# Values of eight key tiles at once, downs in half rows behind the gate/up products, and all output projections after the attention, in a fused attention and GEGLU block

## The chip, the cores and the metric

The kernel runs on one core of one Trainium2 chip. The metric is the device time of one execution in microseconds (us). A core has five engines, each with its own instruction queue: TensorE (PE in the profile; its weight loads are shown apart as PEld), VectorE (DVE), ScalarE (ACT), GpSimd (POOL) and SyncE (SP), which here only issues DMA transfers. The engines meet through semaphores. TensorE's array has 128 rows by 128 columns and can be tiled: a product of 64 rows uses the lower or the upper half of the rows, and two such products, one for each half, can run side by side; a product of 32 columns uses a quarter of the columns.

## The reference

All is fp32, with S = 2048 tokens, D = 576, 32 heads of Dh = 18 and F = 4608 hidden columns:

```
xn = layernorm(x)
s  = MHA(xn)                  # softmax(q k^T * Dh**-0.5) v for 32 heads, then @ wo
g  = silu((gelu(xn @ w_gate) * (xn @ w_up)) @ w_down)
out = x + s * g
```

## The kernel before

**Numbers.** Products of fp32 precision are made from split operands: each fp32 value becomes a high and a low part in TensorE's faster fp32r type, and three products (high x high, high x low, low x high) are summed in PSUM. This holds for the projections, the FFN and the scores. The values (probabilities times V) are plain fp32, on four tiles of 32 columns, one for each of four heads.

**Stages.** A prologue normalises x, transposes it, makes q, k and v and stores them in DRAM. Then comes the long part, one stream of 144 *FFN sections* into which the attention is woven. The tokens are in NB = 4 blocks of TB = 512. In each block the hidden width is cut into NR = 18 row blocks of two 128-wide groups, and one section (`section`, L529) is one group: 27 paired steps of gate and up products (each a pair of 64-row products, one on either half of the array; L393), the split of the next section's weights on GpSimd (`split_gu`), and the activation (`activate`, L403): Square on ScalarE (L406), a multiply-add on VectorE (L407), Copy of `up` on ScalarE (L410) and a product on VectorE (L411), Tanh on ScalarE (L412), a last VectorE step (L414). GpSimd splits its result into `hh` and `hl`, which the downs read.

**The attention.** Its 32 units (four heads by one block of tokens) take four sections each, 128 sections in all (`ATT`, L42). `FIRST` (L41) gives 9 lead sections ahead of them, with so many score pairs each, and 7 are left as the tail. In an attention section `spread` (L56) puts 16 more steps between the 27: 8 pairs of products for the maxima (L787, reduced by VectorE at L788) of a later unit, and 8 pairs of scores (L818), whose exponentials ScalarE takes at L819. Together these are 43 paired steps, called G in the prediction.

**Order behind G in an attention section** (main loop, L914 to L938): the maxima's last steps on VectorE in the third section of a unit (`max_neg`, L790); values of four key tiles (`values`, L844, products at L853); the product that turns the maxima around (`max_end`, L798, L801), also in the third section; the tasks of the output projection; in every second section the downs of the finished row block (`downs`, L560); `finish` (L566), which splits the w_down weights.

**Downs** (`down`, L496). For row blocks other than 0, 1, 16 and 17 all of them come at once in half rows (`half_downs`, L445): eight sums `k` (four token tiles by two halves of D) of six steps each. The upper rows go through the sums in the order 0 to 7; the lower rows start with the last two, 6 and 7, and then take 0 to 5, and step by step one product of the lower rows stands beside one of the upper rows. Both halves of a sum go to the same PSUM bank, so the lower half of sums 0 to 5 may begin only when the upper half has ended. `behind` (L439) sees to that: a tiny ScalarE instruction on a `mark` tile (L441) is made to wait for the last product of the upper half, and the first product of the lower half waits for that mark. `add_down` (L420) adds the finished sum to `Y`: VectorE (L425), or ScalarE for row block 0 (L423). Row blocks 0, 1, 16 and 17 go through the full array, 24 products behind each of two sections (L436 too).

**Output projection.** `load_o` (L592), `norm_o` (L611), `load_wo` (L615), `split_o` (L622) and `project_o` (L651) do it for one block after the other as tasks of single sections, through a schedule written out at L694 to L727. For blocks 0 to 2 the 14 products of one place (128 tokens by 288 columns, L661) are woven into a half-row downs stint; those of block 3 lie in the tail and the epilogue (L941 to L996). `gates` (L511) stores silu's factors of a finished block.

**Who sets the order.** TensorE's order is the program's, by hand. The other engines' order within a section comes from the scheduler, save for single instructions held by `keep_in_program_order`. SyncE issues DMAs in its queue's order. PSUM has eight banks, in tags f (2), m (3) and s (3) (`BANKS`, L45); a matmul that needs a bank waits until its last reader is through.

Of the kernel before, what the change touches and what calls it, by code (L numbers as in the profile page):

```python
# [34 lines left out]
VC = NT // NA  # L35
KB, VB = 7, 2
# [4 lines left out]
FIRST = (0, 0, 4, 6, 6, 6, 6, 6, 6)  # L41
# [10 lines left out]
def f(ap):  # L52
    return ap.bitcast(F32)
# [13 lines left out]
def kernel(ctx: ExitStack, tc: tile.TileContext, x, wqkv, wo, w_gate, w_up, w_down, out):  # L67
# [11 lines left out]
    oT = dram.tile([NQ, P, S], F32, name="oT")  # L79
# [297 lines left out]
    FF = {"w": ahead, "xd": XD, "down": [], "gates": [], "n": 0, "po": None,  # L377
# [42 lines left out]
    def add_down(b, r, py, Y, j, c):  # L420
        yy = Y[:, j, 288 * c:288 * c + 288]
        if r == 0:
            nc.scalar.activation(yy, py, AF.Copy)  # L423
        else:
            nc.vector.tensor_tensor(yy, py, yy, op=ALU.add)  # L425
        if b == NB - 1 and r == NR - 1:
            finals.append((Y, j, c))
# [17 lines left out]
    def half_downs(b, r, hs, wd, Y, po=None):  # L445
# [28 lines left out]
        def out_of(a):  # L474
            bank_o, product_o, _ = po
            for i in range(len(OUT)):
                def step(i=i):
                    product_o(bank_o, i, slice(HR * a, HR * a + HR), a == 0 and i == 0, a == 1 and i == len(OUT) - 1)
                yield step
# [12 lines left out]
    def in_halves(due):  # L492

        return due[-2] and 1 < due[1] < NR - 1

    def down(b, r, hs, wd, Y, js, once):  # L496
        last = len(DOWN) - 1
        if once and 1 < r < NR - 1:
            if js[0] == 0:
                half_downs(b, r, hs, wd, Y, FF["po"] or None)  # L500
# [7 lines left out]
        if b < NB - 1 and r == NR - 1:  # L508
            FF["gates"] += [(b, j, c, Y) for j in js for c in range(2)]

    def gates():  # L511

        for k, (b, j, c, Y) in enumerate(FF["gates"]):
            rows, cc = slice(b * TB + j * P, b * TB + (j + 1) * P), slice(288 * c, 288 * c + 288)
            if j >= 2:
                if c == 0:
                    free = op.tile([P, NK * P], F32, name="th", tag=("oh", "ol")[j - 2])
                th = free[:, 288 * c:288 * c + 288]
            elif k < 3:
                th = op.tile([P, 288], F32, name="th", tag=("yy", "yy", "xx")[k], bufs=(2, 2, 1)[k])  # L520
            else:
                th = ffn.tile([P, 288], F32, name="th")
            tc.keep_in_program_order(nc.scalar.activation(th, Y[:, j, cc], AF.Tanh, scale=0.25))
            nc.gpsimd.tensor_scalar(th, th, 1.0, 1.0, op0=ALU.add, op1=ALU.mult)
            nc.gpsimd.tensor_tensor(th, th, Y[:, j, cc], op=ALU.mult)
            nc.sync.dma_start(ys[rows, cc], th)
        FF["gates"] = []

# [31 lines left out]
    def downs():  # L560
        while FF["down"] and (FF["down"][0][-1] < FF["n"] or FF["n"] == NF):
            down(*FF["down"].pop(0)[:-1])
            if FF["down"] and FF["gates"]:
                gates()

    def finish(pool=ffn, cut=split, bufs=1):  # L566
# [8 lines left out]
        if n % G == G - 1:  # L575
# [9 lines left out]
    op = ctx.enter_context(tc.tile_pool(name="op", bufs=1, reuse_waits="tile"))  # L585
    OT = op.tile([P, NK, TB], F32, name="OT")
    OW = [op.tile([P, NK, 288], F32R, name=name) for name in ("woh", "wol")]
    OG = {}
    OUT = [(k, x, w) for k in range(KT) for x, w in ((0, 0), (0, 1), (1, 0))] + [(KT, 0, 0), (KT, 0, 1)]
    HIND = TB // P - 1  # L590

    def load_o(b, k, pool=op, heads=range(H)):  # L592

        toks = slice(b * TB, (b + 1) * TB)
        if ("den", k) not in OG:
            OG["den", k] = pool.tile([P, TB], F32, name="den")
        den = OG["den", k]
        row, end = k * P, min(D, (k + 1) * P)
        while row < end:
            h, d = divmod(row, DH)  # L600
            m = max(1, (end - row) // DH) if d == 0 else 1
            e = min(DH, d + end - row)
            n = m * (e - d)
            rows = slice(row - k * P, row - k * P + n)
            row += n
            if h in heads:
                nc.sync.dma_start(OT[rows, k, :], oT.rearrange("g (a p) t -> (g a) p t", p=32)[h:h + m, 1 + d:1 + e, toks])
                nc.sync.dma_start(den[rows], rT[h:h + m, toks].rearrange("h (o s) -> h o s", o=1)
                                  .to_broadcast([m, e - d, TB]))

    def norm_o(k):  # L611
        n = min(P, D - k * P)
# [9 lines left out]
    def split_o(i, own=None):  # L622
# [8 lines left out]
        if own:  # L631
            kept.append((oh, ol))
# [392 lines left out]
```

## Time and profile before

| | |
|---|---|
| median of 3 runs | 2572.22 us (2572.05 to 2572.49) |
| the profiled execution's own time | 2571.53 us |
| its span in the trace | 2569.7 us |
| TensorE busy | 2563.5 us |
| VectorE, ScalarE, GpSimd busy | 1973.0, 1573.3, 1366.4 us |
| DMA | 327.34 MB, 127 GB/s on average |
| granted TensorE clock | 1.0 |

The page's first part gives the busy time of each engine, the second the span in 40 slices of 64 us (digits are tenths; PEclk is the granted clock of TensorE). The fourth part follows the chain of work that ended last back to the start. Lines of groups read: line, engine, operation, output <- inputs, shapes, count | busy us in total, mean ns of one | us that the engine was idle before them, and what ended the idle time. Lines of a timeline read: start and length in us, engine, line, operation, count, and in brackets the idle time before and who ended it. A window's line gives start:end, its length, TensorE's busy time and instructions in it, the granted clock, the DMA engines' busy share and the GB/s. Line numbers are those of the kernel before.

### The profile page before, as it was taken

Reading aid. Unit: us, or ns where it says so; the run is one execution under the profiler, and the core shown is the slowest. Engines: PE = TensorE matmul, PEld = TensorE weight load, DVE = VectorE, ACT = ScalarE, POOL = GpSimd, SP = SyncE. Lnnn points to the kernel's source line nnn. Section 1 sums busy time; section 2 is a strip of 40 time slices with the busy share of each in tenths; the row PEclk is TensorE's granted clock in tenths of the full one; section 3 lists DMA queues with packets and bytes.
Section 4 is the critical chain, followed back from the end, with each engine's and each line's share of the span. In section 5 each row is a group of like instructions: output and inputs, shape, how many; then the busy total and the mean of one; then the engine's idle time right before and its main releaser. Section 6 shows DMA issues by size and latency. Waiting matters only on the chain.

```text
span 2569.7 us, 62810 instructions
## 1 busy us (share of the span) xinstructions
PE 2563.5 (100%) x23766; PEld 1930.2 (75%) x23766; DVE 1973.0 (77%) x3502; ACT 1573.3 (61%) x3069; POOL 1366.4 (53%) x1506
## 2 busy tenths in 40 slices
PE   9999999999999999999999999999999999999999
PEld 8888777777777777777777777777777777777778
DVE  5326888888887888787888887878888888788445
ACT  3223466666666676666667766666666766676642
POOL 2117545544566455555457555555455845555663
PEclk9999999999999999999999999999999999999999
DMA  8876444443455444544545454445445543544442
GB/s 266 269 238 159 119 107 102 102 111 97 112 129 140 103 115 99 141 110 114 132 114 138 114 129 115 124 107 136 110 109 127 143 110 104 138 120 111 102 121 57
DMA packets 394940, 327.34 MB, mean 127 GB/s; under 512 B 107980, under 2 KB 308684, under 8 KB 394640
## 3 DMA queue, kind: packets, MB, share of 16 engines
q1 hardware_dynamic: 394640, 323.32, 49.9%
q8 instruction: 190, 3.11, 0.5%
q14 instruction: 110, 0.90, 0.1%
HBM read 269.79 MB, written 52.88 MB: 126 GB/s over the span
## 4 chain that ended last, share of the span: by engine, by line
PE 99%; DVE 0%; DMA 0%; ACT 0%; issue 0%
PE pg L393 26%; PE py L436 18%; PE acc L853 18%; PE pe L818 9%; PE pu L393 9%; PE pm L787 9%; PE po L169 7%; PE po L661 3%; PE pt L230 0%; PE pm L801 0%; DMA xx<-in_A_x_dram 0%; DVE bs L198 0%; ACT xth L177 0%; DVE xx L212 0%; DVE st L202 0%
## 5 line engine op out<-in xcount | busy, mean ns | idle before, releaser
L819 ACT ACTIVATE pT<-pe 128x512 f32<-128x512 f32 x2048 | 1150.8, 598 | 305.7 <-PE pm L787 214.9
L788 DVE TENSOR_REDUCE mx<-pm 128x1 f32<-128x512 f32 x2048 | 1250.8, 680 | 67.8 <-PE pm L787 66.0
L393 PE MATMUL pg<-xd,wh 64*128 64x512 f32 x2592 | 930.6, 391 | 0.0
L393 PE MATMUL pu<-xd,wh 64*128 64x512 f32 x2592 | 929.6, 390 | 0.0
L787 PE MATMUL pm<-KS,q 64*128 64x512 f32 x2048 | 785.2, 388 | 0.0
L818 PE MATMUL pe<-q,KS 64*128 64x512 f32 x2048 | 777.1, 387 | 0.0
L393 PEld LDWEIGHTS pg<-xd,wh 64*128 64x128 f32 x2592 | 476.2, 184 | 105.7 <-issue 29.1
L393 PE MATMUL pg<-xd,wl 64*128 64x512 f32 x1296 | 501.6, 387 | 0.0
L393 PE MATMUL pu<-xd,wl 64*128 64x512 f32 x1296 | 501.4, 387 | 0.0
L393 PEld LDWEIGHTS pu<-xd,wh 64*128 64x128 f32 x2592 | 477.1, 184 | 18.9
L853 PE MATMUL acc<-pT,VS 128*32 128x512 f32 x4096 | 466.0, 595 | 0.0
L102 POOL TENSOR_TENSOR wl<-raw,wh 128x384 fp32r<-128x384 f32 x432 | 436.9, 1024 | 13.6
L100 POOL TENSOR_SCALAR hh<-t 128x512 fp32r<-128x512 f32 x128 | 79.1, 618 | 627.3 <-DVE t L414 615.5
L436 PE MATMUL py<-dh,hh 64*128 64x288 f32 (+1 forms) x1968 | 409.8, 298 | 0.0
L425 DVE TENSOR_TENSOR Y<-py,Y 128x288 f32<-128x288 f32 x544 | 242.3, 456 | 217.9 <-PE py L436 209.2
L787 PEld LDWEIGHTS pm<-KS,q 64*128 64x128 f32 x2048 | 375.6, 184 | 42.8 <-DVE mx L788 5.2
L436 PE MATMUL py<-dh,hl 64*128 64x288 f32 (+1 forms) x1968 | 401.0, 292 | 0.0
L436 PE MATMUL py<-dl,hh 64*128 64x288 f32 (+1 forms) x1968 | 400.9, 292 | 0.0
L818 PEld LDWEIGHTS pe<-q,KS 64*128 64x128 f32 x2048 | 369.8, 184 | 33.5
L853 PEld LDWEIGHTS acc<-pT,VS 128*32 128x32 f32 x4096 | 120.5, 109 | 274.5 <-issue 271.2
L436 PEld LDWEIGHTS py<-dh,hh 64*128 64x128 f32 (+1 forms) x1968 | 273.6, 185 | 39.4 <-DVE t L414 19.3
L100 POOL TENSOR_SCALAR wh<-raw 128x384 fp32r<-128x384 f32 x432 | 218.8, 518 | 107.2 <-DMA raw<-in_B_w_up_dram 59.6
(129 smaller groups left out, 3451.8 us busy)
## 6 DMA issues: line engine op xcount, KB each, us to landing
KS<-qk SPq DMA_DIRECT2D x1536, 36.0 KB
raw<-in_B_w_gate_dram SPq DMA_DIRECT2D x144, 288.0 KB
raw<-in_B_w_up_dram SPq DMA_DIRECT2D x144, 288.0 KB
raw<-in_B_w_down_dram SPq DMA_DIRECT2D x68, 576.0 KB
VS<-vs SPq DMA_DIRECT2D x128, 152.0 KB
qk<-t SPq DMA_DIRECT2D x72, 256.0 KB
q<-qk SPq DMA_DIRECT2D x384, 36.0 KB
xd<-xhs SPq DMA_DIRECT2D x24, 384.0 KB
```

Source lines behind the costliest of these rows:

```text
L100: first = nc.gpsimd.tensor_scalar(hi, raw, 1.0, 1.0, op0=ALU.mult, op1=ALU.mult)
L102: low_part[:] = [keep(nc.gpsimd.tensor_tensor(lo, raw, f(hi), op=ALU.subtract))]
L169: nc.tensor.matmul(o, st, m, start=(i == 0), stop=(i == len(terms) - 1))
L393: nc.tensor.matmul(o, w[1 + wp][k][rr, c, :], xd[xp][k][rr, c, :], start=(i == 0), stop=(i == len(terms) - 1))
L425: nc.vector.tensor_tensor(yy, py, yy, op=ALU.add)
L436: return nc.tensor.matmul(py, hs[g][a][rr, j * P:(j + 1) * P], wd[w][rr, g, 288 * c:288 * c + 288], start=start, stop=stop)
L661: nc.tensor.matmul(po, o[x][rr, k, :], ow[w][rr, k, :], start=start, stop=stop)
L787: nc.tensor.matmul(pm, QS[u, r][rr, t * P:(t + 1) * P], KS[(u * NA + c) % KB][r][rr, :], start=True, stop=True)
L788: nc.vector.tensor_reduce(MX[u][:, 2 * r + a, t, c:c + 1], pm, axis=AX.X, op=ALU.max)
L818: nc.tensor.matmul(pe, KS[(u * NA + c) % KB][r][rr, t * P:(t + 1) * P], QS[u, r][rr, :], start=True, stop=True)
L819: nc.scalar.activation(PT[u, kt][:, 2 * r + a, :], pe, AF.Exp, scale=SCALE)
L853: nc.tensor.matmul(ACC[u][32 * a:32 * a + 32, :], VS[(u * NA + c) % VB][:, v:v + 32], pt[:, a, :], start=first, stop=last, skip_group_chec ...
```

## The change

Seven things are changed together.

1. *Values.* They come in every second attention section, for eight key tiles at once (`VV = 2 * VC`), in one PSUM accumulation where two were added before; `pT` has eight buffers in place of four, and the V tiles of two sections are loaded together.
2. *Downs.* All row blocks of the attention sections go in half rows, also 0, 1, 16 and 17 (63 stints). They come in the sections without values, so that they follow G directly. The upper rows' steps and the lower rows' steps keep their order over the sums; the bank tags are others, and in the last two sums the two halves change places in the stream.
3. *Maxima.* `max_end` makes two products of 64 rows and 64 columns in place of one of 128 rows and 32 columns, in the middle of the half-row downs (after step 32 of 48), and two copies on ScalarE in place of one on VectorE. Its input tile is a zeroed one that stays.
4. *Row block 0* is copied to `Y` by VectorE in place of ScalarE.
5. *Stores of the accumulators.* The sums and the values go to two DRAM tensors, `sT` and `oT`, in five stores for each unit in place of one.
6. *Output projection.* Nothing of it is left among the attention sections. The tail's sections do three places each (6 x 14 = 84 full-array products) between gate/up and downs, the rest follows behind the last section. The weights, `OT`, denominators and `Y` are loaded there, with VectorE doing the products with the denominators and GpSimd the splits. `gates` is gone: `ys` holds `Y` itself, and silu's factors are made in the tail.
7. *Lead and tail.* `FIRST` has ten sections in place of nine, so the tail has six in place of seven.

The core of the diff:

```diff
+VV = 2 * VC
-FIRST = (0, 0, 4, 6, 6, 6, 6, 6, 6)
+FIRST = (0, 0, 4, 4, 4, 4, 6, 6, 6, 6)
...
-            nc.scalar.activation(yy, py, AF.Copy)
+            nc.vector.tensor_copy(yy, py)
...
-    def half_downs(b, r, hs, wd, Y, po=None):
+    def half_downs(b, r, hs, wd, Y, middle=None):
...
-        tags, low = ("sfsfssms", 0) if po else ("ffssmsmm", len(sums) - 2)
+        low = len(sums) - 2
...
-                            pys[k] = bank(tags[k])
-                        begun = a if k < low or po else 1 - a
+                            pys[k] = bank("mmsmfmss"[k])
+                        begun = a if k < low else 1 - a
...
-        if po:
-            rows = [*out_of(0), *downs_of(0, n)], [*downs_of(1, n), *out_of(1)]
-        else:
-            rows = [*downs_of(0, n[low:]), *downs_of(0, n[:low])], [*downs_of(1, n)]
-        for lower, upper in zip(*rows, strict=True):
-            lower()
-            upper()
-        if po:
-            po[2]()
+        rows = [*downs_of(0, n[low:]), *downs_of(0, n[:low])], [*downs_of(1, n)]
+        for i, both in enumerate(zip(*rows, strict=True)):
+            for half in both if i < low * m + m else both[::-1]:
+                half()
+            if middle and i == (low - 1) * m + 1:
+                middle()
...
-        if once and 1 < r < NR - 1:
+        if once:
...
-                once = n in ATT and n + G in ATT and r != NR - 2
+                once = n in ATT and n + G in ATT
...
-            pm = ps.tile([P, P], F32, name="pm", tag="m", bufs=3)
-            nc.tensor.matmul(pm[0:8 * QD, 0:P], NM.pop(u).rearrange("p i c -> p (i c)"), identr, start=True, stop=True)
-            mr = att.tile([8 * QD, P], F32, name="mr", bufs=1)
-            nc.vector.tensor_copy(mr, pm[0:8 * QD, 0:P])
+            pms = [ps.tile([P, TB], F32, name="pm", tag=tag, bufs=BANKS[tag])[:, 0:HR] for tag in tags]
+            for a, pm in enumerate(pms):
+                rr = slice(HR * a, HR * a + HR)
+                nc.tensor.matmul(pm, m2[rr], identr[rr, rr], start=True, stop=True)
+            mr = att.tile([P, P], F32, name="mr", bufs=1)
+            for a, pm in enumerate(pms):
+                nc.scalar.activation(mr[:, HR * a:HR * a + HR], pm, AF.Copy)
...
-            first, last = kt % VC == 0, kt % VC == VC - 1
+            first, last = kt % VV == 0, kt % VV == VV - 1
...
-                nc.sync.dma_start(oT[g, :, cols], acc)
+                nc.sync.dma_start(sT[QD * g:QD * (g + 1), cols], acc.rearrange("(a p) t -> a p t", p=32)[:, 0, :])
+                for a in range(QD):
+                    h = QD * g + a
+                    nc.sync.dma_start(oT[h * DH:(h + 1) * DH, cols], acc[32 * a + 1:32 * a + 1 + DH, :])
...
                 max_neg(um - 1)
-            for kt in range(i * SLOTS // 2, (i + 1) * SLOTS // 2):
-                values(u, kt)
-            load_v(n + 2)
-            if im == 0 and um <= NU:
-                max_end(um - 1)
-            tasks(n, 1)
+                FF["middle"] = lambda u=um - 1: max_end(u)
+            if i % 2:
+                for kt in range((i - 1) * VC, (i + 1) * VC):
+                    values(u, kt)
+                load_v(n + 1)
+                load_v(n + 2)
             downs()
...
+        def load_o(b):
+
+            toks = slice(b * TB, (b + 1) * TB)
+            o = OT[b % 2]
+            nc.sync.dma_start(o[:, 0:KT, :], oT[0:R0, toks].rearrange("(k p) t -> p k t", p=P))
+            nc.sync.dma_start(o[0:HR, KT, :], oT[R0:D, toks])
+            for k in range(NK):
+                den = epi.tile([P, TB], F32, name="den", bufs=2)
...
+                while row < end:
...
+                    nc.sync.dma_start(den[rows], rT[h:h + m, toks].rearrange("h (o s) -> h o s", o=1)
+                                      .to_broadcast([m, e - d, TB]))
+                nc.vector.tensor_tensor(o[0:n, k, :], o[0:n, k, :], den[0:n], op=ALU.mult)
...
+            if n == NU * NA:
+                load_wo()
+                load_o(0)
+                ready(2)
+            elif n < ENDS - 1:
+                for b, j in places[done:done + 3]:
+                    for c in range(2):
+                        put(b, j, c, project_o(b, j, c, "mf"[n % 2]), nc.gpsimd)
+                    done += 1
+                    ready(done + 2)
             downs()
```

`ready(m)` loads (`load_o`), splits (`split_o`) and fetches x and `Y` (`load_xy`) for places up to `m`; `project_o` makes the 14 products of one place and half; `put` multiplies with silu's factor, adds x and stores.

More of the change, by code (lines that the diff above doesn't have):

```diff
@@ L508, in down @@
         if b < NB - 1 and r == NR - 1:
[L509 to L527, printed above, removed]
+            for j in js:
+                nc.sync.dma_start(ys[b * TB + j * P:b * TB + (j + 1) * P, :], Y[:, j])
     def section(specials=(), tag="f", raw_d=None, early=None):
@@ L590 @@
[L590 to L609, printed above, removed]
@@ L975 @@
-        downs()
-        def put(ss, j, cc, add):
-            rows = slice(S - TB + j * P, S - TB + (j + 1) * P)
-            add.tensor_tensor(ss, ss, XX[:, j, cc], op=ALU.add)
-            nc.sync.dma_start(out[rows, cc], ss)
-        late = {}
+        for b, j in places[done:done + 2]:
+            for c in range(2):
+                nc.scalar.activation(S2[:, j, 288 * c:288 * c + 288], project_o(b, j, c, "f"), AF.Copy)
+            done += 1
+            ready(done + 2)
+        downs()
         for Y, j, c in finals:
@@ L984 @@
             cc = slice(288 * c, 288 * c + 288)
[L985 to L996 removed]
+            th = XY[NB - 1, j][1]
@@ L1000 @@
+            gate(th[:, cc], th[:, cc], Y[:, j, cc])
+            if j < 2:
+                put(NB - 1, j, c, S2[:, j, cc], nc.vector)
+        for b, j in places[done:]:
+            for c in range(2):
+                put(b, j, c, project_o(b, j, c, "m"), nc.vector)
 _INS = ['A_x', 'A_wqkv', 'A_wo', 'B_w_gate', 'B_w_up', 'B_w_down']
```

240 lines of the change are left out of this document (79 added, 161 removed).

## The prediction

> **What bounds the kernel now.** I read the head of the page first, then the clock row, the chain that ended last and the GB/s of the slices.
>
> ```profile
> span 2569.7 us, 62810 instructions
> ...
> PE 2563.5 (100%) x23766; PEld 1930.2 (75%) x23766; DVE 1973.0 (77%) x3502; ACT 1573.3 (61%) x3069; POOL 1366.4 (53%) x1506
> ...
> PEclk9999999999999999999999999999999999999999
> ...
> GB/s 266 269 238 159 119 107 102 102 111 97 112 129 140 103 115 99 141 110 114 132 114 138 114 129 115 124 107 136 110 109 127 143 110 104 138 120 111 102 121 57
> ...
> PE 99%; DVE 0%; DMA 0%; ACT 0%; issue 0%
> ```
>
> TensorE is the bound: it is busy for 2563.5 of 2569.7 us, at full clock, and 99% of the chain is its own. So there are two questions: does the change take time out of TensorE's own stream, and does it make TensorE wait anywhere, which it hardly does now? No other engine is near its limit (DVE 77%).
>
> I then cut one unit's stream into its parts (window, us, TensorE busy, clock, DMA share, GB/s).
>
> ```profile
> 374.19:384.17 9.98, 9.98 (x91) 1.00 0.38 100
> 384.17:387.74 3.57, 3.57 (x35) 1.00 0.32 93
> 385.05:386.76 1.71, 1.71 (x20) 1.00 0.31 94
> 387.74:394.22 6.48, 6.48 (x101) 1.00 0.15 35
> 389.96:391.55 1.59, 1.59 (x28) 1.00 0.01 3
> 394.22:404.08 9.86, 9.86 (x90) 1.00 0.46 92
> ...
> 407.65:407.83 0.18, 0.18 (x6) 1.00 0.25 80
> 377.00:379.28 2.28, 2.28 (x22) 1.00 0.30 75
> 262.79:266.17 3.38, 3.38 (x26) 1.00 1.14 221
> ```
>
> In order: gate/up with scores (G, 43 paired steps) behind values; values of four key tiles (V, 8 passes of the four column tiles); the 4 passes in its middle; half-row downs (H, 48 paired steps); 12 steps of H; G behind H; the product of the maxima; 10 steps of G; 24 full-array downs (F). Busy equals window in each: nothing waits.
>
> **The change part by part.** *Fewer changes of the array's tiling.* A pass of V takes 1.71/4 = 0.43 us, so 8 take 3.42, and V has 0.15 over. G behind V takes 9.98 and behind H 9.86, H behind V 6.48 against 48 x 1.59/12 = 6.36: leaving V costs 0.12. A G of 43 steps at 2.28/10 would be 9.80, so some of the 0.06 left belongs to V too. One V stint thus costs 0.27 to 0.33 beyond its passes. The passes stay (128 sections x 8); their stints go from 128 to 64: 64 x 0.27 to 0.33 = −17 to −21; I take −19.
>
> ```profile
> L436 PE MATMUL py<-dh,hh 128*128 128x288 f32 x336 | 102.4, 305 | 0.0
> ```
>
> Full-array downs are 3 x 336 = 1008 matmuls before and 432 after, as blocks 0, 1, 16 and 17 of the hidden width now go in halves too: 576/24 = 24 stints fewer. F is 3.38 against 24 x 1.59/12 = 3.18: 24 x 0.20 = −5. The product of the maxima, 0.18 in another tiling, becomes a pair of 64-column products in H's own tiling, which the trace does not show: between nothing and one paired step of H (0.13); I take 0.08: 31 x −0.10 = −3. The output projection does the same steps in another tiling (a paired half step takes 0.13, like a full one of F: 3.18/24), beside F stints that are there anyhow: 0. **Sum on TensorE: −27**, from −24 to −31.
>
> *Work that other engines lose or gain in the body.* The row-block 0 copies go from ScalarE to VectorE (32 of 0.4 us), the gates, norms and splits of blocks 0 to 2 leave GpSimd and SyncE for the tail, each unit's one store becomes five, the copy of the maxima goes from VectorE to ScalarE in two pieces behind the marks, and one section moves from the tail to the lead without a step more. TensorE did not wait for any of them: 0. If this cover went, the nearest of them, a 0.4 us copy, would cost 31 x 0.4 = 12. VectorE has 32 reductions, eight sums and six gate steps per two sections of some 33 us:
>
> ```profile
> L788 DVE TENSOR_REDUCE mx<-pm 128x1 f32<-128x512 f32 x2048 | 1250.8, 680 | 67.8 <-PE pm L787 66.0
> L425 DVE TENSOR_TENSOR Y<-py,Y 128x288 f32<-128x288 f32 x544 | 242.3, 456 | 217.9 <-PE py L436 209.2
> ```
>
> 32 x 0.68 + 8 x 0.46 + 6 x 0.69 = 29.6 us: it stays under 33.
>
> *The marks.* This is the term that decides. In H the lower half of sum k may begin only when a tiny ScalarE instruction, the mark, has run behind the upper half of sum k. The lower half of sum 0 is step 12, 1.59 us into H. Now H follows V:
>
> ```profile
> 382.94 1.73 ACT L819 ACTIVATE pT<-pe 128x512 f32<-128x512 f32 x3
> 384.57 0.59 ACT L406 ACTIVATE t<-pg 128x512 f32<-128x512 f32 x1
> 385.05 0.61 ACT L410 ACTIVATE t<-pu 128x512 f32<-128x512 f32 x1
> 385.92 0.63 ACT L412 ACTIVATE t<-t 128x512 f32<-128x512 f32 x1 [0.26 <-DVE t L407]
> 388.84 0.20 ACT L441 ACTIVATE mark<-mark 128x1 f32<-128x1 f32 x1 [2.29 <-PE py L436]
> ```
>
> ```profile
> ACT mark L441 <- PE py L436: 299.3, 354, 2.3
> ```
>
> While V runs (384.17 to 387.74), ScalarE finishes the last exponentials and the section's Square, Copy and Tanh, and then sits idle for 2.29 us: the mark is never late, ScalarE waits for TensorE 354 times in 354. After the change H stands where V stood, right behind G. In ScalarE's instruction order of the changed kernel the first mark stands behind Square, Copy and Tanh of the same section in 61 of 63 H stints. Its clock is then Tanh's, and Tanh waits for VectorE. How close an instruction can follow a Tanh, and a TensorE product an activation (start, length):
>
> ```profile
> 229.73 0.62 ACT L412 ACTIVATE t<-t 128x512 f32<-128x512 f32 x1
> 230.25 0.40 ACT L423 ACTIVATE Y<-py 128x288 f32<-128x288 f32 x1
> ```
>
> ```profile
> 10.98 0.60 ACT xth L177
> 11.59 0.04 issue
> 11.63 2.43 PE po L169 x8
> ```
>
> Tanh at 385.92, mark 0.52 later at 386.44, done at 386.64, TensorE 0.05 later at 386.69. Step 12 was due at 384.17 + 1.59 = 385.76. So TensorE waits 0.93 us; H needs no change of tiling behind G, so it starts some 0.1 earlier than V did (out of V's 0.15), and the weight load of a half step comes before its product: 1.1 us. In a section that ends a unit VectorE first has the maxima to finish (404.08 is where values start there):
>
> ```profile
> 404.86 0.22 DVE L793 TENSOR_REDUCE nm<-mx 128x16 f32<-128x64 f32 x1
> ...
> 405.42 0.68 DVE L407 SCALAR_TENSOR_TENSOR t<-t,pg 128x512 f32<-128x512 f32 x1
> ```
>
> ```profile
> 406.13 0.63 ACT L412 ACTIVATE t<-t 128x512 f32<-128x512 f32 x1 [0.56 <-DVE t L407]
> ```
>
> Tanh comes 2.05 behind V's start there and 1.75 in the other: 0.30 more, 1.4 us. **Marks: 32 x 1.1 + 31 x 1.4 = +79**; bounds 63 x 0.93 = +59, and +100 if ScalarE's last exponentials slide too. What is late next: the other five marks and the sums' buffers; ScalarE is free behind the first one and a sum's steps last 0.8 us, a mark 0.2: +2 at most. Who waits for TensorE's delay: VectorE's sums and the next G, which only move along.
>
> *The tail.* All output projections now lie behind the attention: a stint of up to 84 full-array products between G and F in each of the tail's sections.
>
> ```profile
> 2476.41:2482.77 6.36, 6.36 (x56) 1.00 0.11 27
> 2482.77:2486.15 3.38, 3.38 (x26) 1.00 0.12 40
> ```
>
> The first stint is reached after G, F and G behind the last values: 6.36 + 3.38 + 6.36 = 16.1 us. What it needs:
>
> ```profile
> L879 DVE RECIPROCAL rec<-accs 128x512 f32<-128x512 f32 x1 | 3.3, 3344 | 0.0
> L100 POOL TENSOR_SCALAR oh<-OT 128x640 fp32r<-128x640 f32 x28 | 20.2, 724 | 0.2
> L102 POOL TENSOR_TENSOR ol<-OT,oh 128x640 fp32r<-128x640 f32 x28 | 44.1, 1576 | 0.4
> L629 POOL CAST oh<-ol 64x128 fp32r<-64x128 f32 x28 | 7.9, 286 | 1.7
> ```
>
> ```profile
> 2480.27 0.55 SPq L880 DMA_DIRECT2D rT<-rec  x1
> 2481.99 2.19 SPq L608 DMA_DIRECT2D den<-rT  x3
> ```
>
> The sum of the accumulators and the reciprocal end at 1 + 3.3 = 4.3 us; its store is issued in 0.55. Then SyncE, in order: five loads of the projection's weights (2.65 MB), two of OT (1.2 MB), thirteen of denominators (2.19/3 = 0.73 each, through two buffers that VectorE's products free), the next block's fifteen, and only then the next section's gate/up weights. By issue alone: 4.9 + 7 x 0.55 + 13 x 0.73 = 18.2, 1.7 to land (2480.27 to 2481.99, where the next read could go), a product of 0.7, a split of 0.7 + 1.6 + 0.3: 23 us, 7 behind TensorE; by bytes, weights, OT, denominators (1.2) and the gate/up behind them (1.2) are 6.2 MB, 23 us at the 269 GB/s that the page's best slice shows, from 4.9 on: 28, and 6 us of splitting the gate/up weights after that. The two denominator buffers add up to five turns of some 2 us. So the first projection is 7 to 20 us late, and the next G some 5 to 10 behind that; GpSimd's splits and the final buffers add a few. **Tail: +25**, bounds +8 and +38: issue alone, and all of these in a row.
>
> The sum: 2571.5 (the profiled execution's own time; 0.7 below the median 2572.22) − 27 + 79 + 2 + 25 = **2651** us.
>
> *A rule that could overturn it.* The clock row shows 9 in each slice, 1.00 in each window, the start too, where TensorE idles for 2.4 of 14 us:
>
> ```profile
> 0.00:14.00 14.00, 11.61 (x75) 1.00 0.86 228
> ```
>
> The Trainium skill, TensorE: Matmul & The Clock Gate, Part 1, says that an idle window of about 3.4 us halves the clock until a busy one has passed, and its section A second HAM failure mode says that frequent short idles can make it swing. No run here shows either: TensorE never idles now. By the row the sum stays as it is; an estimate by that page, half of a window of 3.4 us lost for each of 63 waits, is +107 us, and without the page the same mechanism is rival (a).
>
> **The rivals.** (a) *The clock swings* with 63 new waits. For: there are none today. Against: 1.1 to 1.4 us in 33 is short, and the start's idle cost no clock. If the 36 steps behind the wait went at half speed, 36 x 1.59/12 = 4.8 us x 63 = +300: about 2950. (b) *The tail's loads are hidden*: 2571.5 − 27 + 79 + 2 = 2626. For: GB/s falls to 57 at the end, so there is room; against: the order of SyncE's queue. (c) *The tail is worse*, each block's fifteen loads holding up each section's weights: +40 to +60, 2666 to 2686. (d) *Faster*: the mark does not hold TensorE, because the upper half's last product, and not Tanh, is what the mark waits for. Its place is step 12 of H, its price 63 x s. With the tail at +8, s = 19/63 = 0.3 us is the point from which it decides; under it the time is below 2571.5; with s = 0 it is 2553, and 2545 without the tail. For it speaks that ScalarE idles 299.3 us before marks; against, that all of this idling lies where V was. (e) That values are not done eight tiles at once: TensorE's instruction order has their products in runs twice as long as before, so no.
>
> **How the numbers follow.** Forecast 0.78; (a) 0.03; (b) 0.08; (c) 0.07; (d) 0.04. The range takes in the marks' and the tail's bounds less their unlikely corners, and (b): 2626 to 2682. Faster and no change come from (d) alone: faster 0.03, within 0.2% 0.01, slower 0.96; 0.2% is about what a measurement of this kernel can tell from no change.
>
> **What would show it.** TensorE's idle time in the body: 63 stretches of 1.1 or 1.4 us, all before a py product at step 12, released by the mark, and the mark starting 0.5 us behind Tanh. V stints of about 7.0 us (3.57 + 8 x 0.43), G between 9.8 and 10.0, F stints 24 fewer. In the tail, TensorE idle before the first po product and then before pg, released by GpSimd's splits and those by DMA. Wrong would be: no wait at step 12; a wait elsewhere in H; a PEclk row below 9; a TensorE busy time that has not fallen by 24 to 31 us.

## The result, and the profile after

The changed kernel takes 2711.56 us (median of 4 runs, 2709.72 to 2714.5), the kernel before beside it 2572.35: 1.0542 times as long, 95% interval 1.0524 to 1.0561. The profiled execution took 2709.72 us with a span of 2707.9, 138.2 us more than before. The forecast was 2651, with a range to 2682: the sign was right, the size was not.

The head of the page, the clock, the GB/s and the chain, as before:

```profile
span 2707.9 us, 63064 instructions
...
PE 2573.5 (95%) x24038; PEld 2014.9 (74%) x24038; DVE 1952.4 (72%) x3470; ACT 1567.7 (58%) x3114; POOL 1289.0 (48%) x1404
...
PEclk9999999999999999999999999999999999999889
...
GB/s 268 255 233 149 87 108 100 98 100 97 100 128 100 100 100 100 100 97 99 98 135 100 98 98 99 96 98 100 97 120 113 100 100 99 100 79 66 156 178 113
...
PE 70%; DVE 20%; DMA 3%; issue 2%; ACT 2%; POOL 2%; SPq 1%; ACTq 0%; POOLq 0%; DVEq 0%
```

TensorE is no longer busy throughout, the clock drops at the end, and the DMA rate of the last slices is higher than before. Of the prediction's own signs of being wrong, two are here: a PEclk row below 9, and a TensorE busy time that rose by 10 us where it was to fall by 24 to 31. Busy time counts a product at half clock as longer, and an H as 6.63 us where it takes 6.37 without the wait (e1). The waits of TensorE (who waits, for whom: us, times, longest):

```profile
PE py L438 <- ACT mark L443: 62.8, 63, 1.2
PE po L846 <- DVE thl L853: 25.9, 5, 10.3
PE po L846 <- POOL oh L102: 21.0, 1, 21.0
PE pu L395 <- POOL xd L139: 13.0, 5, 3.8
```

There are three groups: 63 waits for marks, which were forecast; waits of the output projection in the tail, forecast at less than half their size; and five waits of gate/up for `xd`, which the forecast does not have at all.

**The body.** The windows of one pair of sections (values of eight tiles, G behind it, H, G behind H, and an H with the maxima's product):

```profile
430.22:437.22 7.00, 7.00 (x66) 1.00 0.65 140
437.22:447.11 9.89, 9.89 (x91) 1.00 0.45 128
447.11:454.62 7.51, 6.63 (x100) 1.00 0.27 79
454.62:464.49 9.87, 9.87 (x90) 1.00 0.44 86
412.42:420.34 7.92, 6.74 (x100) 1.00 0.17 46
```

V is 7.00, as worked out (3.57 + 8 x 0.43). H is 7.51 and 7.92 in place of 6.36. The first row is 1.15 us too long by the wait alone; the second 1.56, of which 0.26 is the maxima's products (e1, below) and 1.3 the wait. Within them TensorE is idle for 0.88 and 1.18 us. ScalarE and TensorE at the start of the first of these H:

```profile
448.95 0.63 ACT L414 ACTIVATE t<-t 128x512 f32<-128x512 f32 x1 [0.26 <-DVE t L409]
449.49 0.42 ACT L443 ACTIVATE mark<-mark 128x1 f32<-128x1 f32 x2
```

```profile
448.56 0.29 PE L438 MATMUL py<-dh,hl 64*128 64x288 f32 x2
449.73 0.40 PE L438 MATMUL py<-dh,hh 64*128 64x288 f32 x2 [0.88 <-ACT mark L443]
```

The mark starts 0.54 behind Tanh, and step 12 starts 1.17 behind step 11 instead of 0.13.

**The block changes.** Three G stints, at 747, 1375 and 2002, take 16.4 to 16.9 us and not 9.9. The first of them in pieces:

```profile
747.51:753.21 5.70, 4.60 (x42) 1.00 1.06 193
757.00:760.26 3.26, 0.00 (x0) 1.00 0.40 116
760.47:763.89 3.42, 3.42 (x18) 0.50 0.02 5
```

TensorE idles for 1.1 us, then for 3.5 (from 756.72 on), and then runs 3.42 us at half clock. This is where `xd`, the tokens of the next block, is loaded anew.

**The tail.** From the last values to the end of the last product it takes 187.8 us (2516.59 to 2704.35). TensorE's unstalled stints of the same trace, six G of 6.37, seven stints of downs (26.1 in all) and 448 projection steps of 0.133, give 123.9: 64 us too much, of which 53 are idle and the rest is for the most part half clock.

```profile
2532.90:2553.74 20.84, 0.00 (x0) 0.00 (x1) 5.42 (x8) 1.18 (x2) 0.78 (x2) 0.56 0.66 184
2553.74:2577.95 24.22, 15.19 (x84) 14.64 (x85) 8.54 (x12) 2.57 (x4) 17.86 (x21) 0.74 0.73 202
2588.86:2610.90 22.05, 14.86 (x85) 14.30 (x85) 12.28 (x18) 4.75 (x7) 11.34 (x11) 0.77 0.53 153
2620.56:2643.67 23.11, 12.83 (x86) 12.63 (x85) 8.50 (x14) 3.00 (x5) 13.07 (x15) 0.78 0.60 188
```

Here the windows have all engines (TensorE, its loads, VectorE, ScalarE, GpSimd). The first is the idle time ahead of the first projection; the other three are projections of 84 products, which take 11.2 us unstalled.

### The profile page after: what moved, and what is told of

Its sections match the earlier page's. It is cut to its first block, busy times and chain, and to the rows that moved or that the text cites. A ratio compares the mean times of both kernels' runs of the same rounds, so it can differ in the third digit from the quotient of the medians.

```text
span 2707.9 us, 63064 instructions
## 1 busy us (share of the span) xinstructions
PE 2573.5 (95%) x24038; PEld 2014.9 (74%) x24038; DVE 1952.4 (72%) x3470; ACT 1567.7 (58%) x3114; POOL 1289.0 (48%) x1404
## 4 chain that ended last, share of the span: by engine, by line
PE 70%; DVE 20%; DMA 3%; issue 2%; ACT 2%; POOL 2%; SPq 1%; ACTq 0%; POOLq 0%; DVEq 0%
DVE mx L624 18%; PE pg L395 17%; PE acc L693 16%; PE py L438 14%; PE po L171 7%; PE pe L658 6%; PE pm L623 5%; PE pu L395 3%; DVE t L409 1%; PE po L846 1%; DMA den<-rT 1%; ACT t L408 1%; DMA xd<-xhs 1%; ACT pT L659 1%; DMA yy<-ys 1%
## 5 line engine op out<-in xcount | busy, mean ns | idle before, releaser
L693 PE MATMUL acc<-pT,VS 128*32 128x512 f32 x4096 | 452.8, 594 | 0.0
L438 PE MATMUL py<-dh,hh 64*128 64x288 f32 (+1 forms) x2160 | 351.0, 299 | 65.0 <-ACT mark L443 62.8
L438 PE MATMUL py<-dh,hl 64*128 64x288 f32 (+1 forms) x2160 | 344.3, 294 | 0.0
L693 PEld LDWEIGHTS acc<-pT,VS 128*32 128x32 f32 x4096 | 127.3, 110 | 289.9 <-issue 276.2
L438 PE MATMUL py<-dl,hh 64*128 64x288 f32 (+1 forms) x2160 | 342.3, 292 | 0.0
L427 DVE TENSOR_TENSOR Y<-py,Y 128x288 f32<-128x288 f32 x544 | 235.2, 455 | 136.5 <-PE py L438 136.4
L438 PEld LDWEIGHTS py<-dh,hh 64*128 64x128 f32 (+1 forms) x2160 | 219.3, 185 | 88.2 <-ACT mark L443 77.3
```

What stands on the lines that cost most here:

```text
L438: return nc.tensor.matmul(py, hs[g][a][rr, j * P:(j + 1) * P], wd[w][rr, g, 288 * c:288 * c + 288], start=start, stop=stop)
L693: nc.tensor.matmul(ACC[u][32 * a:32 * a + 32, :], VS[(u * NA + c) % VB][:, v:v + 32], pt[:, a, :], start=first, stop=last, skip_group_chec ...
```

## The experiments

Theory: three waits, independent of each other, lie on TensorE: the mark behind Tanh, the late reload of `xd`, and SyncE's queue in the tail. The rival to each stands in its expectation.

**e1, the first mark ahead of Tanh.** `activate` leaves Copy and Tanh of a section with half-row downs to `half_downs`, which issues them behind the first and the second mark:

```diff
                             elif a == 1:
                                 seen[k] = behind(one)
+                                if FF.get("late"):
+                                    FF["late"].pop(0)(seen[k])      # Copy, then Tanh, ordered behind the mark
```

> The changed kernel with one edit: in the sections whose downs are in half rows, ScalarE takes Square, first mark, Copy, second mark, Tanh, in place of Square, Copy, Tanh, first mark. Nothing is left out. Theory (the first mark is late because it stands behind Tanh): TensorE's waits before step 12, some 84 us in 63 stints (a stint of 7.51 or 7.92 us against 6.36 unstalled), fall to 0 to 0.3 us each: 65 to 84 us less, 2628 to 2647. Rival (the lower half waits for the upper half's own result to arrive, or for a bank that VectorE frees, and the mark's place in the queue matters little): a gain under 20 us, above 2690.

Measured: 2641.54 us, ratio to the kernel before 1.0266 (1.0251 to 1.0281). That is 70 us less, inside the theory's interval; the rival falls. An H of this run, without and with the maxima:

```profile
377.63:384.00 6.37, 6.37 (x100) 1.00 0.31 92
410.77:417.40 6.63, 6.63 (x100) 1.00 0.21 54
```

The wait before step 12 is gone. The second row shows what the maxima's products cost in H: 0.26 us.

**e2, without the reload.**

```diff
-        if n + 1 < NF and (n + 1) % (NR * G) == 0:
-            FF["xd"] = load_xd(b + 1)
```

> The changed kernel with the activations xd of the first block of tokens kept for all four blocks: it leaves out the three reloads of xd (loads and GpSimd copies), so blocks 1 to 3 use the first block's tokens in gate/up. Theory (the three gate/up stints of 16.4 to 16.7 us at the block changes wait for the reload): they fall to 9.9 us, 13 us of idle time and 7 us at half clock behind it: 20 us less, about 2692. Rival (they wait for the weights' splits on GpSimd, which have the same place in the queue): under 5 us, above 2706.

Measured: 2692.48 us, ratio 1.0464 (1.0449 to 1.0480), 19 us less: the three stints are the reload's, idle time and half clock together.

**e3, values of four tiles again.**

```diff
-VV = 2 * VC
+VV = VC
...
-            if i % 2:
-                for kt in range((i - 1) * VC, (i + 1) * VC):
-                    values(u, kt)
-                load_v(n + 1)
-                load_v(n + 2)
+            for kt in range(i * VC, (i + 1) * VC):
+                values(u, kt)
+            load_v(n + 2)
```

> The changed kernel with one part undone: values of four key tiles behind every attention section again, in every second section ahead of the half-row downs. Nothing is left out. Theory: the values stint covers ScalarE's Tanh again, so the first marks are early and 84 us go; 64 more values stints cost 17 to 21 us in changes of tiling: 2645 to 2649. Rival (the marks are late for another reason than the place of the downs): 17 to 21 us more, about 2731.

Measured: 2665.59 us, ratio 1.0361 (1.0346 to 1.0377), 46 us less and not 63 to 67. The rival's sign is wrong: the marks are early as soon as values stand between G and H, and no wait for a mark is left in the trace. The size was missed for two reasons that the trace shows: the marks were worth 70 and not 84, and the waits for `xd` grew, to 19.7 us from 13.0:

```profile
PE pu L395 <- POOL xd L139: 19.7, 14, 3.6
```

The second of these tells something more: with H behind values again, where it stood before, the reload is at least as late as in the changed kernel. That H follows G directly is not what delays it.

**e4, another order of the tail's loads.**

```diff
-                load_wo()
                 load_o(0)
+                load_wo()
...
-                if j == 0 and b + 1 < NB:
-                    load_o(b + 1)
                 split_o(b, j)
                 load_xy(b, j)
+                if j == 1 and b + 1 < NB:
+                    load_o(b + 1)
```

with `den` in four buffers.

> The changed kernel with another order of SyncE's loads in the tail: OT and denominators of block 0 ahead of the projection's weights, each later block's OT and denominators behind the second place's x and Y of the block before in place of ahead of the first one's, and four denominator buffers in place of two. Nothing is left out. Theory (the order of SyncE's queue sets the tail's waits: 21.0 us before the first projection, 7.3 to 10.3 us before banks whose reader waits for Y): 30 to 45 us less, 2667 to 2682. Rival (the bytes set them, whatever the order): 10 us less at most, above 2700.

Measured: 2696.18 us, ratio 1.0475 (1.0457 to 1.0492), 15 us less, between the two. The wait for the first projection fell from 21.0 to 13.6 us, but 8.9 us now stand before a G. Its weights are issued behind the denominators, at 2560.6, and by the list of waits the last thing it waits for is a bank that VectorE frees.

**e5, the reload asked for earlier.** `load_xd` in thirds, each as soon as gate/up has read the old one:

```diff
+            upto(9)
+            new = load_xd(b + 1, None, [0])
         nxt = load_gu((n + 1) % (NR * G), keep) if n + 1 < NF else None
```

> The changed kernel with one edit: at the three block changes each third of xd is asked for as soon as gate/up has read the old one for the last time, the first third ahead of the next section's weights in SyncE's queue. Nothing is left out. Theory (the reload is late because its loads stand in SyncE's queue behind a weight load that waits for a raw buffer): the loads start some 3 us sooner and go ahead of key loads; the wait of 4.6 us in each of the three stints falls to 0 to 2 and the half clock behind it goes: 10 to 20 us less, 2692 to 2702. Rival (GpSimd's order, its copies standing behind other splits, sets it): under 5 us, above 2706.

Measured: 2712.67 us, ratio 1.0543 (1.0527 to 1.0559): nothing. It told nothing of the theory either: the scheduler put the loads into the same order as without the edit, and the first one was issued at 737.0 (736.7 before the edit). e9 and e10 force the order.

**e6, the same order, one place later** (`j == 2` in e4's last line).

> The changed kernel with e4's order of the tail's loads and one step more: a later block's OT and denominators come behind the third place of the block before, so that the next section's gate/up weights stand ahead of them. Nothing is left out. Theory (the order moves the wait to whatever stands last in SyncE's queue; in e4 that was the gate/up weights, 8.9 us and a half clock stint of 12.2 us): 10 to 20 us less than e4's 2696, 2676 to 2686. Rival (13 issues of denominators for each block hold up what follows wherever they stand): within 5 us of e4, 2691 to 2701.

Measured: 2695.34 us, ratio 1.0476 (1.0460 to 1.0491). The rival holds: of these two places for the denominators neither is better, some load is behind them in both.

**e7, five loads of denominators for a block in place of thirteen**, on top of e6:

```diff
+            nc.sync.dma_start(rX[QD * DH * g:QD * DH * (g + 1), j * TB:(j + 1) * TB].rearrange("(h d) s -> h d s", d=DH),
+                              rt.rearrange("h (o s) -> h o s", o=1).to_broadcast([QD, DH, TB]))
...
-                while row < end:
...
+                nc.sync.dma_start(den[0:n], rX[row:end, toks])
```

> e6 with the denominators repeated 18 times in DRAM by one more transfer for each unit, so that a block's denominators are five loads of whole tiles in place of thirteen, through four buffers. Nothing is left out. Theory (SyncE's issues, some 0.8 us each, set the tail's waits): the first projection's wait falls from the 13.6 us of e4 to some 5 and the later ones nearly go: 15 to 30 us less than e6, 2650 to 2670. Rival (bytes: 2.65 MB of weights, 1.2 MB each of OT and denominators before the first projection): within 5 us of e6.

Measured: 2685.81 us, ratio 1.0442 (1.0427 to 1.0458), 10 us less than e6, between theory and rival. The first projection still waits 11.9 us. Issues are a part of it and not all.

**e8, e1, e5 and e7 together.**

> The changed kernel with the first mark ahead of Tanh (e1), the early reload (e5) and the tail of few loads (e7) together. Nothing is left out. Theory (the three waits lie one behind the other on TensorE and add): the gains of e1 (70), e5 and e7 add up, 2575 to 2600. Rival (a wait removed uncovers another): over 2610.

Measured: 2617.37 us, ratio 1.0177 (1.0160 to 1.0194), 94 us less. The time lies where the rival put it, over 2610, but not for the rival's reason: the gains add (70 + 26 + 0 = 96), and e5 had none to add.

**e9, GpSimd's order at the block change**: its last copy of `xd` ahead of the low part of the hidden values and of the next weights.

```diff
+                if k == 0 and n > G and n % (NR * G) == 0:
+                    behind_xd(first, 1)              # no wait, only the order on GpSimd
```

> e5 left SyncE's order as it was, so it told nothing of the order. This is the changed kernel with GpSimd's order alone edited: at the block changes its last copy of xd comes ahead of the split of the hidden values' low part and of the next weights, which stand ahead of it now. Nothing is left out. Theory (of the 4.6 us that each of these stints waits, 3.5 are GpSimd's order, and they bring a window of half clock): 12 to 18 us less, 2694 to 2700. Rival (the last third of xd lands only then, so the copy can't start sooner): under 5 us, above 2706.

Measured: 2704.14 us, ratio 1.0513 (1.0497 to 1.0528), 7 us less, between theory and rival. TensorE's waits for `xd` fall from 13.0 to 3.9 us.

**e10, and the loads of `xd` ahead of the weight load in SyncE's queue.**

> e9 and SyncE's order too: the loads of xd ahead of the weight load that waits for a raw buffer. Nothing is left out. Theory (the rest of the wait is the loads' late start): the 1.1 us goes too, 17 to 22 us less than the changed kernel, 2690 to 2695, as far as e2 without any reload came. Rival (bytes: the reload takes some 17 us from its first load on wherever it starts): as e9.

Measured: 2692.87 us, ratio 1.0469 (1.0452 to 1.0487), 18.7 us less, the time of e2, which does not reload at all. SyncE's order is worth 11 of it on top of e9's 7, not the 1.1 us of the theory. SyncE and GpSimd in this run:

```profile
734.06 4.64 SPq L146 DMA_DIRECT2D xd<-xhs  x4
740.63 1.25 SPq L146 DMA_DIRECT2D xd<-xhs  x2
```

```profile
747.68 1.47 POOL L147 CAST xd<-xd 64x1536 fp32r<-64x1536 f32 x1 [0.74 <-DMA xd<-xhs]
749.49 1.47 POOL L147 CAST xd<-xd 64x1536 fp32r<-64x1536 f32 x1 [0.35 <-PE pe L671]
```

In the changed kernel the loads and the last copy look like this:

```profile
735.25 0.66 SPq L122 DMA_DIRECT2D raw<-in_B_w_gate_dram  x1
...
736.69 1.26 SPq L138 DMA_DIRECT2D xd<-xhs  x2
```

```profile
732.55 2.67 POOL L104 TENSOR_TENSOR dl<-raw,dh 128x1152 fp32r<-128x1152 f32 x1
...
758.75 1.46 POOL L139 CAST xd<-xd 64x1536 fp32r<-64x1536 f32 x1
```

In the kernel before, the split of w_down comes behind the last copy, and the first two loads come ahead of the weight load:

```profile
747.91 1.47 POOL L137 CAST xd<-xd 64x1536 fp32r<-64x1536 f32 x1 [0.88 <-DMA xd<-xhs]
749.47 0.62 POOL L100 TENSOR_SCALAR hh<-t 128x512 fp32r<-128x512 f32 x1
750.05 1.16 POOL L100 TENSOR_SCALAR dh<-raw 128x1152 fp32r<-128x1152 f32 x1
```

```profile
729.69 1.31 SPq L136 DMA_DIRECT2D xd<-xhs  x2
731.84 0.60 SPq L120 DMA_DIRECT2D raw<-in_B_w_gate_dram  x1
```

The chain reads: all downs of row block 16 now end with the H at 730.63, where the kernel before did half of them one section later (740.26 to 743.58). GpSimd splits the next w_down weights right behind that H (until 735.2); only then a raw buffer is free and the weight load at the head of SyncE's queue is issued (735.25); `xd` stands behind it. The last copy comes at 758.75, 9.3 us later than in e10 and 11.2 behind the start of the new block's first G (747.51); in the kernel before it is 4.3 behind (743.58). e3 and e16 fit this: e3 has H behind values, row block 16 in halves, and the waits; e16 has row blocks 0, 1 and 17 in halves, keeps row block 16 as before, and has none. No run gives row block 16 alone its old place in the changed kernel.

**e11, the tail's queues cleared**: on top of e7, VectorE's products with the denominators ahead of the next activation, output stores through GpSimd's queue, projection weights by halves.

```diff
-            nc.sync.dma_start(out[b * TB + j * P:b * TB + (j + 1) * P, cc], th[:, cc])
+            (nc.sync if add is nc.vector else add).dma_start(out[b * TB + j * P:b * TB + (j + 1) * P, cc], th[:, cc])
```

> e7 with the tail's queues cleared: VectorE takes the products of block 0 with the denominators ahead of the next section's activation, the output stores of the tail's sections go through GpSimd's DMA queue and no longer stand in SyncE's, the projection's weights are loaded by halves, three buffers for Y. Nothing is left out. Theory (instructions that wait at the head of a queue, VectorE's activation and SyncE's stores, hold up loads that are ready): the first projection waits 3 to 6 us in place of 11.9, the later waits nearly go: 15 to 25 us less than e7's 2686, 2661 to 2671. Rival (bytes and GpSimd's splits): within 6 us of e7.

Measured: 2699.57 us, ratio 1.0494 (1.0478 to 1.0509), 14 us more than e7, which neither theory nor rival had. The first projection's wait fell (6.5 us and smaller ones behind it), but new waits stand before downs, whose banks VectorE frees late:

```profile
PE py L442 <- DVE Y L431: 9.3, 3, 4.7
```

VectorE has silu's factor of a later place at the head of its queue there, which waits for ScalarE's Tanh. By the trace that Tanh waits for Y ahead of the first of the three, and ahead of the other two for an output store of `thl`, the tile it writes.

**e12, e1, e10 and e11 together.**

> The changed kernel with the first mark ahead of Tanh (e1), the reload's orders (e10) and the cleared tail (e11). Nothing is left out. Theory (the waits add): 70 + 20 + 40 to 50 us less than the changed kernel, 2572 to 2582, level with the kernel before at best, since about 30 us of waits stay in the tail. Rival (a wait removed uncovers another): over 2595.

Measured: 2607.28 us, ratio 1.0135 (1.0120 to 1.0150): 104 us less than the changed kernel, where 70 + 19 + 12 = 101 were measured one by one. The time is in the rival's range, over 2595, but the waits add; the miss is e11's. No version of the change came down to the kernel before.

**e13, e14, e15: what of the tail is whose.**

```diff
-                nc.vector.tensor_tensor(o[0:n, k, :], o[0:n, k, :], den[0:n], op=ALU.mult)   # e13: and its loads
...
-                nc.sync.dma_start(yy, ys[rows, :])                                           # e14
-                gate(th, th, yy)
+                gate(th, th, xx)
```

> The changed kernel without the denominators in the tail: it leaves out their 52 loads and 20 products on VectorE, so that unnormalised heads are projected. Theory (SyncE's order with 13 denominator loads for each block sets most of the tail's 53 us of waits and 12 of half clock): the first projection waits 3 to 8 us in place of 21, the later waits of 7 to 10 us go for the greater part: 35 to 50 us less, 2662 to 2677. Rival (bytes of weights and OT, and the chain from Y over Tanh to the bank): under 20 us, above 2692.

> The changed kernel without the 12 loads of Y in the tail: it leaves them out and computes silu's factor from x, with the same instructions otherwise. Theory (the waits of 7.3, 5.1, 2.1 and 10.3 us before products that need a bank are the chain Y, Tanh, product, bank, and Y's load stands behind the next block's denominators): 10 to 20 us less, 2692 to 2702. Rival (x's load and the output stores stand in the same queue, so the chain is as late without Y): under 5 us, above 2706.

> e13 and e14 together: no denominators and no loads of Y in the tail. Theory (the two account for nearly all of the tail's waits): 50 to 62 us less than the changed kernel, 2650 to 2662. Rival (weights, OT and GpSimd's splits hold the rest): e13's time within 5 us.

Measured: 2682.06 us (ratio 1.0426, 1.0412 to 1.0441), 2707.37 (1.0525, 1.0511 to 1.0540) and 2674.77 (1.0398, 1.0384 to 1.0412): 29.5, 4 and 37 us less. e13 falls between its theory and its rival, e14 as the rival said, and e15 fits neither. The denominators (52 loads and 20 products, left out together) are the greatest single part, Y's loads a small one, and about 26 of the 64 us have neither to do with it: in e15 the first projection still waits 7.4 us in two pieces, and 9.8 us in smaller ones and some 9 us of half clock follow. By the list of waits GpSimd's splits end all of these. What is left to hold them, or the splits ahead of them, are weights, OT, x and the output stores; how these share the 26 stays open.

**e16, half rows for row blocks 0, 1 and 17 in the kernel before.**

```diff
-        return due[-2] and 1 < due[1] < NR - 1
+        return due[-2]
...
-        if once and 1 < r < NR - 1:
+        if once:
```

> The kernel before with one part of the change alone: the downs of row blocks 0, 1 and 17 in half rows too, where an attention section follows (18 full-array stints fewer, row block 16 stays). Nothing is left out. Theory (a full-array stint costs 0.20 us for the array's two changes of tiling): 18 x 0.20 = 3.6 us, 3 to 6 us less than the kernel before, about 2568. Rival (the halves' marks or the order at the block changes cost more): no gain, 2572 or more.

Measured: 2571.38 us beside 2572.32, ratio 0.9997 (0.9987 to 1.0006): no difference that can be told from none. The medians are 0.9 us apart; the interval reaches from 3.3 us less to 1.5 more. The kernel before shows why:

```profile
757.13:763.71 6.58, 6.58 (x53) 1.00 0.72 178
723.24:726.62 3.38, 3.38 (x28) 1.00 0.24 59
```

The first row is a stint of 48 full-array products, two in one, and there are nine like it. Against an H behind V, 6.48, it loses 0.1 us and not 0.4.

## Why the prediction was right or wrong

The forecast was 60 us short. In the traces the change is +138.2: 74 for the marks, 64 for the tail, 20 for the reload and −20 for the tiling. The forecast had +79 and 2, +25, 0 and −27.

- **"TensorE did not wait for any of them: 0"** is one of the two steps that failed. It missed the reload, +20 (19 by e2 and e10; 13.0 us idle, the rest half clock). All downs of row block 16 now come in one section, so GpSimd's split of the next w_down weights comes ahead of the copies of `xd`; the split frees a raw buffer, and the buffer starts a load that stands ahead of `xd` (e9, e10; e3 and e16 for row block 16). The reload was not looked at as something that the moved step is queued before; the sum only asked whether the engines had time.
- **Tail, +25 (8 to 38)** is the other one: it measured 64. The first wait came as forecast, behind SyncE's loads in their order, and ended with GpSimd's split; it was 21.0 us against 7 to 20. The 5 to 10 us before the next G did not come (0.9). Five waits, 26 us, for a bank that VectorE had not freed were put at "a few", and the idle stretches cost clock as well, 11 us. By e13 nearly half of the 64 is the denominators'; some 26 stay open. Rival (b), that the loads are hidden, is refuted. Rival (c), worse by 40 to 60, had 0.07 and came nearest in size, but its place, each section's weights, is not where TensorE waits.
- **Tiling, −27: too large**, it was about −20. The term of the values stints was right, −20 where −19 was said, counted over the stints of the traces: V 64 x (2 x 3.57 − 7.00) = −9, all G together −5 (9.98 to 9.89 behind V), and the 51 H that stood behind V −6 (6.48 to 6.37; the 24 with projection products 8.33, of which 14 x 0.133 are those). The term of the full-array stints, −5, was wrong: they were counted as 24 single ones at 0.20, and 18 of them stood in pairs, 6.58 a pair, 0.2 over an H behind G, so 9 x 0.2 and 3 x 0.4 make −3. The maxima's −3 had the wrong sign: 0.26 us in H (e1) against 0.18 before is 31 x 0.08 = +2.5; 0.26 lies outside both of its bounds, 0 and 0.13. Taking the single experiments (70 for e1) in place of the stints leaves −15 for all of it.
- **Marks, +79: right**, place, mechanism, the two sizes (1.1 and 1.4 forecast, 1.15 and 1.3 measured; the idle time within them is 0.30 us apart, as forecast) and the count of 63. The 63 H take 486 us in the changed kernel and 411 in e1: 74. e1 gained 70 net, since its stints at the block changes are 4 us longer. Rival (d), that the mark would not hold TensorE, is refuted by the same run.
- **The clock.** Rival (a) said that 63 waits of 1.1 to 1.4 us would make it swing. They did not: it is 1.00 in every H window. It fell elsewhere, mostly behind idle stretches of over 3 us, and cost some 7 us at the block changes and 11 in the tail, which no term had. The Trainium skill, TensorE: Matmul & The Clock Gate, Part 1, has this: an idle window of about 3.4 us halves the clock. The trace agrees at the first block change, 0.50 for 3.42 us behind 3.54 idle; elsewhere less was enough, as the last section shows.

## What to carry to other kernels

When a step is moved, follow each buffer that it frees to the load which waits for that buffer, and that load to everything behind it in its queue: one split that came ahead of the copies cost some 20 us on TensorE. Work that is moved to an end with nothing beside it needs its loads and its buffers counted to the last one, since every wait there lies on the path; one lag is not the sum. A price for a stint's two changes of tiling is only worth what the neighbours of that stint make of it, so count the stints as they stand in the stream.

## What the hardware showed unexpectedly

The half clock comes in windows of 3.41 us. In the tail, behind 20.8 us of idle time:

```profile
2535.41:2553.74 18.33, 0.00 (x1) 0.50 0.60 164
2553.74:2559.30 5.56, 3.79 (x14) 0.50 0.44 128
2559.30:2569.54 10.24, 5.80 (x44) 1.00 0.62 141
2569.54:2576.37 6.83, 4.02 (x17) 0.50 1.09 318
```

After the first products the clock stays at half for 5.6 us; it is back for 10.24, three times 3.4, and falls again for 6.83 in and behind the next idle stretch of 7.3 us. In this way idle time costs more than its own length.

An idle stretch as long as a window isn't needed. All changes of the clock in a trace lie on one grid of 3.41 us, and the traces of the changed kernel and of e1 to e15, cut along it, show what counts: how long TensorE was busy, by the trace, within one window. Up to 1.52 us busy, half clock followed each time; from 1.53 to 1.91, sometimes; from 1.92 on, never. It came back behind a window with 2.83 us or more busy, and stayed at half behind 2.81 or less. A wait of 0.88 or 1.18 us leaves over 2.2 us busy, which is why the 63 of them cost no clock. In e9, at the second block change, a window with no idle stretch over 1.8 us fell below:

```profile
1380.38:1383.79 3.41, 3.40 (x35) 1.00 0.50 134
1383.79:1387.20 3.41, 1.63 (x24) 1.00 0.00 0
1387.20:1390.62 3.42, 3.42 (x32) 0.50 0.77 246
```

And a load took longer to land where more was under way: the first denominators of the tail took 10.88 us by the chain of waits, the later ones 4.4 and 4.2, with 296 GB/s moved meanwhile against 152 and 115. That the traffic is the cause isn't shown.

```profile
2528.48 10.88 DMA den<-rT
...
2541.73 4.39 DMA den<-rT
...
2547.73 4.20 DMA den<-rT
```
